# Dummy products on TensorE and earlier weight conversion in the opening of a DeltaNet and feed-forward kernel

## The chip, the cores and the metric

The kernel runs on one core of one Trainium2 chip. The metric is the device time of one execution in microseconds, the median of several runs. The engines work side by side, each through its own stream of instructions in order: TensorE (PE: matrix products; PEld: the loading of their weights), VectorE (DVE), ScalarE (ACT), GpSimd (POOL) and SyncE (SP, which issues DMAs here). TensorE's results go to PSUM, whose banks the kernel hands out in three pools.

## The reference

Two blocks follow each other. The first is a DeltaNet recurrence over 768 steps, for 4 batches and 8 heads of size 48; the second is a feed-forward block of 3072 tokens, 384 to 2048 to 384, with a sigmoid-gated activation.

```python
k_n = k / (np.linalg.norm(k, axis=-1, keepdims=True) + 1e-06)
for t in range(S):
    y[:, :, t] = np.einsum('bhd,bhde->bhe', q[:, :, t], state)
    v_old = np.einsum('bhde,bhd->bhe', state, kt)
    state = state + bt[:, :, :, None] * np.einsum('bhd,bhe->bhde', kt, vt - v_old)
...
h = x @ w_in
g = h * (1.0 / (1.0 + np.exp(-1.702 * h)))
return (g @ w_out)
```

The inputs of attention are fp32; both weight matrices reach the kernel as 64-bit floats and are converted to fp32 on the chip.

## The kernel before

**Tiling.** The sequence is cut into 6 chunks of 128 steps; a chunk of one batch (8 heads) is a unit, so there are 24 units, numbered chunk by chunk. In a unit the recurrence becomes a triangular system. Its Gram matrix of the keys is computed by `gram` (line 375: eight products into two tiles named psG, each copied to the tile G by ScalarE). The 32x32 diagonal blocks are inverted by `invert` (line 441) on VectorE, for all heads of several batches at once, in 15 growing steps of a product and a sum (tiles P and YB) and, from chunk 1 on, 8 larger ones and a pass through DRAM. In chunk 0 the last part is done by TensorE instead (`joined`, line 531: psZ, a copy by ScalarE, psC, then the tiles YT and XB on VectorE). Then the four blocks of a unit are solved one after the other.

**Hops.** `together` (line 816) is the body of a hop: for one unit, `solve` multiplies a block of V by its inverse (psU), copied to U by ScalarE; for the other, `below` multiplies the block solved in the hop before into the rows beneath (psR), which VectorE subtracts from V. Two units take turns, so that the first chunk's four units make two pairs, each with 8 hops. The first pair's hops are the loop at line 1036, the second pair's the one at line 1074. Beside each hop stands something else: the rest of `joined`, the transposes and score products of other units (psT, psQ), the Gram products of chunk 1 (`preparing`). When a pair is solved, `put_out` (line 997) computes the outputs (psY), and `state` (line 679) adds the unit's part to the state ST on VectorE (line 690) out of the same bank as part of psY. ScalarE copies psY to xT, the input of the feed-forward block. These banks and those of psU, psR and half of psQ come from one pool of four, `ps_seq`; psG of chunk 0, the products of the feed-forward block and the dummies from a pool of two, `ps_moe`.

**Dummy products.** `warm(n)` (line 132) issues n products of a 128x128 identity with 128x256 bf16 values into a tile ps_warm that nobody reads. NW = 14 stand at the very start, NY = 30 behind the Gram products (line 983), and `warm(NU // 2 if i < 6 else NA)`, 5 or 3, at the end of each hop of the first pair; NU = 11 in the first three hops of the second.

**Conversion.** `conversion` (line 205) turns a piece of a weight matrix from 64 to 32 bits in five VectorE steps (tiles w_in or w_out and tmp) and one of ScalarE. `conversions` (line 255) strings the pieces together, with the first step of a piece put among those of the piece before; `fill(n)` (line 294) issues the next n steps. The pieces of w_in come in four quarters: two pieces of 768 elements per partition, two more, three of 512, two of 768. Pieces of w_out follow, mostly of 384. When certain pieces are done, DMAs fetch more raw weights into the freed places.

**What sets the order.** The order on each engine of this part is written out by hand and kept in program order. `fill(1)` stands in each hop of the first pair, `fill(2)` behind each of its two `put_out`; `fill(2)` or `fill(3)` in each hop of the second pair, with `feed()`, which issues three products of the hidden layer (ph), from the fourth hop on; `feed()` and `fill(3)` behind each `put_out`. Then a loop (line 1097) issues two steps and one `feed()` per round until the last piece of w_in is done; then come the 25 steps of `invert(1)`, one `feed()` with each, then `fill(5)`. The rest of the conversion is issued within `both_written` (line 761, po), which waits for w_out piece by piece; from there on `woven` (line 860) interleaves the remaining units with the feed-forward block.

```python
    for i in range(2 * NB):
        together(*next(path))
        beside_hops[i]()
        fill(1)
        if i > 1:
            ahead_of(preparing, 1)
...
        warm(NU // 2 if i < 6 else NA)
    for n, s in enumerate(pair[:2]):
        put_out(s)
        load(len(KN) + n, ((KN, k),), other_queue)
        fill(2)
```

## Time and profile before

| | us |
|---|---|
| median of 3 runs | 781.13 (780.93 to 782.76) |
| the profiled execution | 784.58 |
| its span, first to last instruction | 782.9 |
| PE busy | 752.8 (96%) |
| VectorE busy | 449.1 (57%) |
| ScalarE busy | 242.0 (31%) |
| mean granted clock of TensorE | 0.964 |
| DMA moved | 50.80 MB |

The page of a profile gives the busy time of each engine, then the span in 40 slices with the busy share in tenths and the TensorE clock that was granted, in tenths of full speed. Other answers of the same trace give the busy time and the clock in any stretch, the instructions of an engine in order of time (start, duration, operation, tiles written and read, shapes, and in brackets the idle time just before with what ended it), and the chain of work that ended last, where "issue" is time in which an engine waited for nothing that the profile shows. A matrix product in fp32 appears as two records. Ends of products are modelled, so a busy PE isn't always PE at its peak.

### The profile page before, as it was taken

The numbers are of one execution on the slowest core, as the hardware profiler recorded it, in microseconds if no ns is written. First come the engines' busy times: TensorE is split into PE (matmuls) and PEld (weight loads), VectorE is DVE, ScalarE is ACT, GpSimd is POOL, SyncE is SP. The second block draws the span as 40 slices with busy tenths as digits, with TensorE's granted clock in tenths as the row PEclk, the third lists the DMA queues.
The fourth block names the chain that finished last, engine by engine and source line by source line (L and its number), as shares of the span: only waits on it lengthen the run. The fifth ranks groups of instructions, "written<-read, shape, count | busy, mean of one in ns | idle before, by whom it ended". The sixth has DMA issues, their size and how long they took to land.

```text
span 782.9 us, 19754 instructions
## 1 busy us (share of the span) xinstructions
PE 752.8 (96%) x8625; PEld 564.8 (72%) x8625; DVE 449.1 (57%) x922; ACT 242.0 (31%) x539; POOL 127.0 (16%) x133
## 2 busy tenths in 40 slices
PE   7889999688999999999999999999999999999997
PEld 5677788355678678678678678678678678687674
DVE  6747889996977666666666666666655531000000
ACT  4445652243333223223223123123123123121110
POOL 6112510011121221221221221231200000000000
PEclk8657999999999999999999999999999999999999
DMA  9931941463332141141141142142130020000000
GB/s 175 168 62 45 201 123 33 115 166 85 76 94 63 38 98 49 39 97 51 36 97 50 36 98 53 33 98 55 31 77 12 23 44 1 15 13 1 26 1 21
DMA packets 130662, 50.80 MB, mean 65 GB/s; under 512 B 105408, under 2 KB 126016, under 8 KB 130576
## 3 DMA queue, kind: packets, MB, share of 16 engines
q1 hardware_dynamic: 128112, 41.08, 23.9%
q0 software_dynamic: 2464, 8.46, 4.2%
q8 instruction: 68, 1.11, 0.6%
q14 instruction: 18, 0.15, 0.1%
HBM read 32.08 MB, written 16.25 MB: 62 GB/s over the span
## 4 chain that ended last, share of the span: by engine, by line
PE 83%; DVE 12%; issue 2%; ACT 1%; DMA 0%; POOL 0%; DVEq 0%; POOLq 0%; ACTq 0%; SPq 0%
PE po L102 29%; PE ph L102 27%; PE psU L102 6%; PE psY L102 5%; PE psQ L102 4%; PE psG L102 4%; PE psT L102 3%; DVE P L102 3%; PE ps_warm L102 2%; DVE w_out L102 2%; DVE YB L102 2%; PE psR L102 2%; DVE tmp L102 2%; DVE NT L102 1%; DVE V L102 1%
## 5 line engine op out<-in xcount | busy, mean ns | idle before, releaser
L102 PE MATMUL po<-w_out,gT 128*128 128x384 f32 x768 | 267.4, 497 | 9.6 <-ACT ksq L102 5.1
L102 PE MATMUL ph<-xT,w_in 128*128 128x256 f32 x1152 | 261.2, 383 | 0.3
L102 PEld LDWEIGHTS ph<-xT,w_in 128*128 128x128 f32 x1152 | 214.9, 190 | 32.5 <-issue 1.7
L102 PEld LDWEIGHTS po<-w_out,gT 128*128 128x128 f32 x768 | 142.0, 192 | 101.5 <-DVE w_out L102 7.8
L102 DVE TENSOR_TENSOR V<-V,psR 64x384 f32<-64x384 f32 (+1 forms) x96 | 53.3, 556 | 199.2 <-PE psR L102 198.0
L102 ACT ACTIVATE gT<-ph 128x512 f32<-128x512 f32 x96 | 56.4, 595 | 138.9 <-PE ph L102 138.8
L102 DVE TENSOR_TENSOR P<-NT,YB 64x18 f32<-64x18 f32 (+25 forms) x186 | 86.3, 464 | 5.4
L102 PEld LDWEIGHTS psU<-V,XB 32*32 32x32 f32 x1536 | 61.0, 109 | 36.8 <-issue 29.6
L102 ACT COPY US<-psU 32x384 f32<-32x384 f32 x92 | 43.2, 469 | 142.4 <-PE psR L102 124.0
L102 DVE TENSOR_REDUCE YB<-P 64x6 f32<-64x18 f32 (+25 forms) x186 | 77.7, 418 | 6.4
L102 PE MATMUL psU<-V,XB 32*32 32x48 f32 x1536 | 72.3, 208 | 2.6 <-issue 1.7
L102 PE MATMUL psR<-US,G 32*32 32x48 f32 x2208 | 64.0, 209 | 2.1 <-issue 2.1
L625 POOL TENSOR_SCALAR_AFFINE_SELECT M<-M 128x1024 f32<-128x1024 f32 x20 | 25.2, 1258 | 248.3 <-DVE M L102 170.4
L102 PEld LDWEIGHTS psR<-US,G 32*32 32x32 f32 x2208 | 54.3, 110 | 3.4 <-issue 2.8
L102 PE MATMUL psQ<-QS,kT 48*128 48x176 f32 (+1 forms) x384 | 36.2, 329 | 1.3 <-ACT QS L102 0.9
L102 PE MATMUL psG<-kT 48*128 48x128 f32 x384 | 32.5, 308 | 3.8 <-ACT kT L102 1.7
L102 PEld LDWEIGHTS psG<-kT 48*128 48x128 f32 x384 | 27.5, 208 | 7.3 <-ACT kT L102 2.1
L102 PEld LDWEIGHTS psQ<-QS,kT 48*128 48x128 f32 x384 | 29.7, 198 | 3.7 <-ACT QS L102 1.5
L102 ACT COPY o<-po 128x384 f32<-128x384 f32 x24 | 11.5, 478 | 61.8 <-issue 39.2
L102 DVE TENSOR_TENSOR P<-NT 64x256 f32<-64x256 f32 (+7 forms) x36 | 30.3, 842 | 0.4
L102 DVE TENSOR_REDUCE NT<-P 64x64 f32<-64x1024 f32 (+7 forms) x36 | 29.3, 814 | 1.2
L87 POOL DMA_DIRECT2D KN<-in_k_dram x13 | 12.4, 953 | 104.9 <-PE psY L102 96.0
(106 smaller groups left out, 629.1 us busy)
## 6 DMA issues: line engine op xcount, KB each, us to landing
Nd<-G SPq DMA_DIRECT2D x16, 512.0 KB, 3.4
V<-in_v_dram SPq DMA_DIRECT2D x24, 192.0 KB, 3.0
QP<-in_q_dram SPq DMA_DIRECT2D x24, 192.0 KB, 3.8
out_dram<-o SPq DMA_DIRECT2D x24, 192.0 KB, 2.1
KN<-in_k_dram POOLq DMA_DIRECT2D x15, 192.0 KB, 3.7
NT<-Nd SPq DMA_DIRECT2D x20, 128.0 KB, 2.6
Yd<-YS SPq DMA_DIRECT2D x20, 128.0 KB, 2.4
XB<-Yd SPq DMA_DIRECT2D x20, 128.0 KB, 3.1
```

What stands on the lines that cost most here:

```text
L87: dma(out=dst[n % len(dst)][:, :, 0:D], in_=src[b, :, c * C : (c + 1) * C, :].rearrange("h p d -> p h d"),)
L102: return lambda *a, **kw: tc.keep_in_program_order(op(*a, **kw))
L625: (pool if self.n < B else nc.gpsimd).affine_select(out=self.M, in_=self.M, compare_op=ALU.is_gt, fill=0.0, base=0, pattern=[[0, H], [1, 1 ...
```

## The change

Two things change, all of it in the first 110 us of the program. Dummy products: eight behind each of the four Gram computations of chunk 0 and eight behind the transpose of the first unit's queries, into a bank of `ps_seq`; 40 in place of 30 behind them; 11 in place of 5 in hops 0 to 5 of the first pair. Conversion: two steps in place of one in each hop of the first pair; three steps within each of the four `put_out`, between the state products and the state addition, in place of the two or three behind it. The steps themselves stay the same, and so does their order.

```diff
-    NW, NA, NY, NU = 14, 3, 30, 11
+    NW, NA, NY, NU, NG = 14, 3, 40, 11, 8
-    def warm(n, after=None):
-        ps = ps_moe.tile([128, 256], F32, tag="moe", name="ps_warm")
+    def warm(n, pool_=ps_moe, tag="moe"):
+        ps = pool_.tile([128, 256], F32, tag=tag, name="ps_warm")
...
-        def state(self, psS=None):
+        def state(self, psS=None, between=None):
...
+            if between:
+                between()
             St = ST[:, self.b, 0 : NP * D].rearrange("p (j d) -> p j d", j=NP)
             vec.tensor_tensor(St, psS, St, op=ALU.add)
...
+    def warm_beside(n):
+        warm(n, ps_seq, "seq")
+
     for b in range(HB):
         gram(b)
+        warm_beside(NG)
     pair = [new_step(n) for n in range(HB)]
+    next(pair[0].scored)
+    warm_beside(NG)
     run(pair[0].scored)
     pair[0].select()
     for b in range(HB, B):
         gram(b)
+        warm_beside(NG)
...
-        fill(1)
+        fill(2)
         if i > 1:
             ahead_of(preparing, 1)
...
-        warm(NU // 2 if i < 6 else NA)
+        warm(NU if i < 6 else NA)
     for n, s in enumerate(pair[:2]):
-        put_out(s)
+        put_out(s, lambda: fill(3))
         load(len(KN) + n, ((KN, k),), other_queue)
-        fill(2)
...
     for s in pair[2:]:
-        put_out(s)
+        put_out(s, lambda: fill(3))
         feed()
-        fill(3)
```

In the instruction order of the changed kernel the loop at line 1097 issues nothing any more, and all of its `feed()` and of the later ones, 25 in all, stand beside the inversion of chunk 1. Apart from that, only line numbers differ.

## The prediction

> **What bounds the kernel now.** I read the busy shares in slices first, then the same in stretches of 4 and 20 us, then the order of time of VectorE and TensorE between 12 and 190 us, then the chain.

> ```profile
> PE   7889999688999999999999999999999999999997
> DVE  6747889996977666666666666666655531000000
> PEclk8657999999999999999999999999999999999999
> ```

> A slice is 19.6 us. From the eleventh slice on PE is full at full clock, and the edit touches nothing there, so this steady part can't change; what can move is when it begins, about 186 us. The first four slices run at a reduced clock (0.8, 0.6, 0.5, 0.7); in slices 7 to 9 VectorE is full and PE falls to 6 and 8.

> ```profile
> 12.00:16.00 4.00, 3.13 (x85) 2.79 (x86) 3.72 (x8) 1.08 (x2) 0.97 (x2) 0.66 1.03 208
> 24.00:28.00 4.00, 3.67 (x22) 3.15 (x23) 3.86 (x5) 2.25 (x8) 1.36 (x3) 0.50 1.12 171
> 28.00:32.00 4.00, 4.00 (x33) 2.92 (x34) 3.93 (x4) 2.92 (x13) 0.00 (x0) 0.71 1.20 148
> 36.00:40.00 4.00, 3.03 (x110) 2.39 (x113) 1.41 (x3) 0.57 (x2) 0.00 (x0) 0.65 1.11 156
> 48.00:52.00 4.00, 4.00 (x124) 3.18 (x123) 1.65 (x3) 2.16 (x6) 1.09 (x1) 0.50 0.01 4
> 56.00:60.00 4.00, 4.00 (x105) 3.06 (x103) 2.33 (x6) 2.57 (x10) 1.68 (x1) 0.50 0.02 4
> 68.00:72.00 4.00, 3.65 (x80) 3.34 (x76) 3.15 (x5) 2.38 (x8) 1.94 (x3) 1.00 0.22 57
> ```

> The columns are PE, PEld, DVE, ACT, POOL, granted clock, DMA. Up to 32 us VectorE is full (the inversion of chunk 0) and PE waits for it. In the hops of the first pair (34.7 to 66 us) it is the reverse: PE 4.00 of 4.00 at clock 0.50, VectorE about half idle. In half-microsecond stretches the clock falls at 13.3, rises at 30.4, falls at 37.2, rises at 67.9.

> ```profile
> 35.31 1.66 issue
> 40.65 2.08 issue
> ```

> In the chain PE twice waits for nothing the profile shows, in hops 0 and 1; each time one of the 16 KB instruction transfers was under way while DMA was over 100% busy.

> ```profile
> 120.00:140.00 20.00, 20.00 (x94) 17.62 (x93) 18.77 (x37) 4.78 (x8) 0.00 (x0) 1.00 0.01 2
> 140.00:160.00 20.00, 12.05 (x56) 6.44 (x56) 19.42 (x35) 5.08 (x8) 1.91 (x1) 0.91 0.51 132
> 160.00:180.00 20.00, 17.98 (x178) 10.88 (x174) 19.31 (x44) 8.45 (x18) 2.96 (x2) 1.00 0.54 143
> ```

> From 105 to 141 us PE is full with the first two batches' hidden products; from 141 to 185 us VectorE (97%) sets the pace with the w_out conversion, and PE idles 5.15 us at 141.24.

> **Step 1, Gram stage: five times 8 dummies, and 40 for 30.** All of it lies in front of the first psZ, which needs the transpose YT of VectorE's inversion, 28.83 plus 1.97 = 30.80. Today PE's thirty dummies run to 32.0. A dummy took 0.213 us at 0.50 (sixteen in 26.95 to 30.36) and 0.12 at 1.00 (eleven in 1.31). Fifty more cost 6.0 us at 1.00 and 10.7 at 0.50; waits of 0.67 us three times cover 2.0. What decides is the clock. I count the time of products that fill the 128x128 array. The stretch that raised the clock at 30.4 held nothing else; the one before 67.9 held 1.11 of psT, 0.85 of dummies and most of psY's 1.87. Hop 2 (45.3 to 50.0) had 2.08 of psQ (48 of 128 rows) and 1.25 of dummies and did not rise, so narrow products count by their rows. Now 8 dummies (1.7 us) follow each gram (1.7 to 2.6 us, at 48/128), and two groups stand around a psT: 80 to 90% of a 3.4 us stretch by this count, where 66% (20.1 to 23.5 today) did not suffice and 91% did (3.05 to 6.5). I take a rise by 23.5. Then grams take 1.09 instead of 2.56, and the 40 dummies end between 29.5 and 33.3: psZ from 1.1 us earlier to 1.3 later. I take 0.

> **Step 2, the hops.** Hops 0 to 5 issue 11 dummies instead of 5: 6 x 0.213 = 1.28 us more each at 0.50 (PE is full, nothing hides it), 0.72 at 1.00. At 1.00 the rest of a hop halves (psU and psR 1.1 to 0.55, psZ or psC 1.27 to 0.65), so PE needs 0.55 + 0.65 + 1.31 = 2.5 us against today's 3.42. In hop 1, psT (1.11) and the dummies (2.35 at 0.50) stand side by side, 3.46 us of full-array products; hop 2 has psQ and 2.35. The stretch with these reaches some 80%, so I take a rise near 47 to 48 us. It stays up: 11 dummies are 1.31 of at most 3.4 us, 38% and over; stretches with as much stayed at 1.00 (72 to 79 us).

> [...]

> With the clock up, VectorE becomes the hops' bound. From the subtraction of hop 1 to the second state addition it has: subtractions 2 x 1.14 + 4 x 0.56 = 4.5; YT and XB 2 x 0.71 = 1.4; normalizing 2 x 0.54 + 0.92 = 2.0; state additions 2 x 0.36 = 0.7; 18 conversion steps on 768 elements (0.69 to 0.96, mean 0.90) and 2 on 512 (0.42) = 17.0; sum 25.7 us.

> ```profile
> 61.74 0.56 DVE L102 TENSOR_TENSOR V<-V,psR 32x384 f32<-32x384 f32 x1 [1.00 <-PE psR L102]
> 65.83 0.55 DVE L102 TENSOR_REDUCE ssq<-ksq 128x8 f32<-128x384 f32 x1
> 68.64 0.36 DVE L102 TENSOR_TENSOR ST<-psY,ST 128x192 f32<-128x192 f32 x1 [2.27 <-PE psY L102]
> ```

> The 2.27 us ahead of the first state addition now hold three steps. What waits behind these is the addition, and behind it the second pair's first psU, which needs the bank: 68.7 against 69.86 today. Hop 1's subtraction starts at 43.35 now; 1.28 of dummies more, less up to 2.08 if the instruction wait falls where PE idles anyway: 42.6 to 44.6, I take 43.8. Add 25.7 and 1.9 of waits (1.5 in hop 2, before the clock rises): second addition done at 71.4, with 22 steps done. Before stands at 73.2 with 12 (71.48 and two steps). **Gain 1.8**; bounds: loss 5 (cold throughout, rival A) to gain 7 (no waits, no instruction stall, rival C).

> **Step 3, second pair.** As many steps as before (10 + 9 + 6 = 25), in front of the additions at 102.4 and 105.4, where VectorE idled 2.26 and 0.95. PE's last psY (105.35) moves with step 2: 103.5.

> **Step 4, loop and inversion.** ("in", 3, 1) is done at step 46 (1 + 9 x 5). Before stands at 37 and makes five rounds (105.7 to 117); after stands at 47 and makes none, so 25 feeds fall beside the 25 steps of inversion. PE: from the last psY to the end of the hidden products 35.9 us (105.35 to 141.24), the same products. VectorE: psQ subtractions at about +3, inversion 27.4 (117.11 to 144.5), done at +31: the bound passes to PE. The first tail item (ssq, now 146.60 = 105.35 + 41.25) waits for ScalarE behind the last gT: 35.9 + 0.25 + 0.60 + 0.61 + 0.51 = +37.9. **Gain 3.4.** It is 0 if PE's feeds are held or the NT transfers (last issued at 110.12, 2.4 to land) stay there; 5 at best (PE's idle gap). The fetches of the weights move earlier, to a time at 0 to 2% DMA.

> **Step 5, tail.** Same steps, VectorE-bound, 0.

> Sum 1.8 + 3.4 = 5.2. The profiled execution took 784.58 (span 782.9 and 1.7 around it), so 779.4; the median of the three is 3.45 lower: 775.9, said as 776.

> **Rivals.** A, the clock stays at 0.50 through the hops (or rises after hop 4): hops 0 to 5 grow by 1.28 each, 7.7 in all; of this 2.7 return (the two steps behind the second addition, 1.9, and part of the 2.27 in front of the first); less 3.4 from step 4: +1.6, 782.7; with a late rise 778 to 780. For it: a hop of 4.7 us has only 2.35 of full-array products. Against: hops 1 and 2. B, on the other side: the Gram stage stays at 0.50. Then 10.7 less 2.0 less what 32.0 - 30.8 spares leaves psZ 7.5 late; the instruction waits (3.7) fall into that time, and the hops and step 4 are as in A: 781.1 + 7.5 - 3.7 + 1.6 = 786.5; 790 if the waits remain, 783 if the hops warm up. It decides if no stretch before 24 us raises the clock, that is if more than 90% is needed. C, more gain: the clock is up in hop 0 and neither instruction wait returns: 3.7 + 1.5 less than the forecast, 771. D, the steps do not run early since raw weights or ScalarE's part of a step are late: no gain in steps 2 to 4, 780 to 781; against it DMA at 0 to 2% from 48 us and ScalarE 2.2 of 4 busy.

> [...]

> **Numbers.** Forecast 0.50 (own range 773 to 779), A 0.19, B 0.13, C 0.13, D 0.05. 770 to 785 leaves out the ends of B and C. A difference under 0.3% (2.3 us) can't be told from none. Faster: forecast, C and the late part of A, 0.69; same 0.17; slower 0.14.

> **What would show it.** Clock 1.00 before 24 us and again by 51; hop period near 2.8 with VectorE over 85% busy from 48 to 72; state additions near 68.5 and 71; inversion's first product right behind the psQ subtractions, near 107; no PE gap at the end of ph; first po near 139.5. Wrong if the clock is 0.50 in the hops, if psZ starts after 33.5, or if the inversion waits for NT.

## The result and the profile after

The changed kernel takes 784.85 us (median of 12 executions, 781.92 to 786.86), the kernel before 782.24 beside it (780.50 to 784.17): ratio 1.003, 95% interval 1.0013 to 1.0047. A second measurement (e5 below) gave 1.0001. The forecast was 776, so the expected gain is missing; the question is where it went. The profiled execution took 786.75, its span 785.0.

The page of the changed kernel, busy tenths and granted clock in slices of 19.6 us:

```profile
PE   8697999888999999999999999999999999999997
...
DVE  6677689896977666756656666666665531000000
...
PEclk8878899999999999999999999999999999999999
```

The clock did rise: slices 2 to 4 have 0.8, 0.7 and 0.8 where before had 0.6, 0.5 and 0.7, and VectorE's third slice is a 7 where it was a 4. But PE has a 6 in the second slice and a 7 in the fourth, and the fifth slice of the clock is an 8 where it was a 9. The same stretches as before, and those where the new holes are (PE, PEld, DVE, ACT, POOL, clock, DMA):

```profile
28.00:32.00 4.00, 3.35 (x170) 2.80 (x167) 3.38 (x2) 1.37 (x6) 0.00 (x0) 1.00 1.18 149
32.00:36.00 4.00, 0.00 (x0) 0.00 (x0) 0.00 (x0) 0.00 (x0) 0.00 (x0) 0.86 0.86 146
...
48.00:52.00 4.00, 4.00 (x148) 3.50 (x142) 2.72 (x4) 2.32 (x7) 1.13 (x1) 0.94 0.13 22
...
68.00:72.00 4.00, 1.41 (x37) 1.28 (x33) 3.93 (x7) 1.48 (x5) 2.86 (x3) 1.00 0.11 27
72.00:76.00 4.00, 4.00 (x33) 3.34 (x31) 2.81 (x8) 2.68 (x8) 3.79 (x6) 0.55 0.80 249
76.00:80.00 4.00, 4.00 (x77) 3.31 (x76) 0.46 (x1) 1.48 (x3) 0.28 (x1) 0.50 1.04 270
```

At 28 us the Gram stage is warm, as forecast (1.00 where it was 0.71). Then no engine does anything between 32 and 36 us. From 48 us on the hops are warm. At 68 to 72, the border between the two pairs, VectorE works 3.93 of 4 and PE 1.41; behind that the clock is down to 0.5 and it is VectorE that idles (0.46). So there are two new holes.

**Hole 1** in the chain of waits (start, duration, what):

```profile
31.53 0.39 PE psC L102 x23
31.92 4.67 issue
36.59 0.76 PE psC L102 x38
```

PE stops in the middle of the 64 products of the first psC, for nothing that the profile shows, and VectorE's YT and XB, on which everything in hop 0 rests, wait behind it:

```profile
37.37 0.29 DVE L102 TENSOR_TENSOR YT<-YT,psC 128x128 f32<-128x128 f32 x1 [5.99 <-PE psC L102]
37.69 0.42 DVE L102 TENSOR_TENSOR XB<-YT,U 128x256 f32<-128x256 f32 x1
```

Before, the first XB stood at 34.18, 1.6 us behind the end of the inversion; now it is 6.3 us behind it. Behind PE's idle time the clock falls at 34.85, for 13.7 us.

**Hole 2**, the order of time at the border on ScalarE, PE and VectorE:

```profile
70.33 0.72 ACT L102 ACTIVATE w_in<-w_in,low 128x512 int32<-128x512 int32 x1 [2.46 <-DVE w_in L102]
...
71.11 0.54 ACT L102 COPY xT<-psY 128x256 f32<-128x256 f32 x2
...
73.06 0.54 ACT L102 COPY xT<-psY 128x256 f32<-128x256 f32 x2 [1.24 <-DVE ST L102]
```

```profile
68.29 0.65 PE L102 MATMUL psY<-US,KN 128*64 128x48 f32 x16
71.54 0.86 PE L102 MATMUL psU<-V,XB 32*32 32x48 f32 x16 [2.59 <-ACT xT L102]
72.33 2.38 PE L102 MATMUL psQ<-QS,kT 48*128 48x128 f32 x16
```

```profile
70.21 0.35 DVE L102 TENSOR_TENSOR ST<-psY,ST 128x192 f32<-128x192 f32 x1
...
79.54 1.14 DVE L102 TENSOR_TENSOR V<-V,psR 32x384 f32<-32x384 f32 x2 [4.66 <-PE psR L102]
...
86.14 1.14 DVE L102 TENSOR_TENSOR V<-V,psR 32x384 f32<-32x384 f32 x2 [3.55 <-PE psR L102]
```

The second pair's first psU waits 2.59 us, and what ends the wait is ScalarE's copy of psY to xT (71.11). Two things stand ahead of that copy. One is VectorE's addition to ST (70.21, done at 70.56), behind VectorE's three steps: the copy reads the bank that also holds the state products, and it waits for the addition, as the like copy of the second unit (73.06) shows. The other is the conversion's step in ScalarE's own queue (70.33), which waited 2.46 us for VectorE's steps. After the standstill the clock falls at 72.40 for 10.2 us, and PE's psQ and dummies run at half speed.

Further on, the inversion of chunk 1 gives back what was forecast, nearly: ssq is 38.7 us behind the last psY (41.5 before).

To compare kernels I use five marks of each trace: first XB behind the end of the inversion; hop 1's subtraction behind the first XB; the end of the second state addition behind this; the last psY of the second pair behind that; first ssq of the tail behind the last psY. All but the inversion and the addition count by their starts. Only profiled executions have them, one for each kernel. When the second state addition begins, the kernel before, e3 and e12 have done 10 steps of the conversion, e1, e7, e10 and e14 19, the others 22; so the column ST compares only kernels with equally many.

| kernel | XB | hop 1 | ST | psY | ssq | span | ratio to before, 95% |
|---|---|---|---|---|---|---|---|
| before | 1.6 | 9.2 | 28.1 | 33.6 | 41.5 | 782.9 | |
| after | 6.3 | 6.8 | 28.5 | 36.6 | 38.7 | 785.0 | 1.0030 (1.0013 to 1.0047) |
| e1 steps behind | 4.1 | 7.3 | 26.6 | 32.8 | 38.7 | 776.8 | 0.9977 (0.9951 to 1.0003) |
| e2 border dummies | 5.1 | 6.6 | 27.1 | 32.3 | 38.7 | 778.3 | 0.9979 (0.9962 to 0.9995) |
| e3 dummies only | 4.8 | 6.8 | 23.9 | 33.7 | 41.5 | 778.3 | 0.9951 (0.9936 to 0.9966) |
| e4 conversion only | 1.2 | 7.6 | 29.5 | 32.3 | 38.7 | 776.5 | 0.9966 (0.9946 to 0.9987) |
| e5 changed again | 3.3 | 6.8 | 28.6 | 34.7 | 38.7 | 781.6 | 1.0001 (0.9979 to 1.0024) |
| e6 hop dummies | 1.2 | 6.2 | 29.2 | 33.9 | 38.7 | 778.2 | 0.9997 (0.9973 to 1.0021) |
| e7 behind, kept warm | 5.0 | 6.8 | 26.6 | 33.2 | 38.7 | 780.1 | 0.9978 (0.9957 to 0.9998) |
| e8 late fetch | 5.8 | 6.8 | 29.7 | 32.3 | 38.7 | 781.8 | 1.0023 (0.9999 to 1.0047) |
| e9 wide dummies | 1.4 | 9.4 | 29.3 | 34.6 | 38.7 | 781.2 | 0.9959 (0.9933 to 0.9984) |
| e10 joined best | 1.2 | 7.4 | 25.4 | 32.8 | 38.7 | 772.7 | 0.9916 (0.9886 to 0.9947) |
| e11 copies first | 5.5 | 6.8 | 28.8 | 30.5 | 38.7 | 777.3 | 0.9948 (0.9923 to 0.9972) |
| e12 Gram dummies | 5.8 | 5.6 | 28.1 | 36.8 | 41.5 | 785.0 | 1.0026 (0.9997 to 1.0055) |
| e13 both mended | 1.2 | 7.4 | 27.3 | 32.1 | 38.7 | 774.7 | 0.9926 (0.9903 to 0.9949) |
| e14 joined, tail | 1.2 | 8.2 | 28.4 | 32.8 | 38.7 | 775.6 | 0.9923 (0.9897 to 0.9949) |

### The profile page after: what moved, and what is told of

Same layout as the page of the kernel before. It is cut to its first block, busy times and chain, and to the rows that moved or that the text cites. A ratio compares the mean times of both kernels' runs of the same rounds, so it can differ in the third digit from the quotient of the medians.

```text
span 785.0 us, 19920 instructions
## 1 busy us (share of the span) xinstructions
PE 754.9 (96%) x8711; PEld 566.3 (72%) x8711; DVE 447.2 (57%) x922; ACT 242.0 (31%) x539; POOL 127.9 (16%) x133
## 3 DMA queue, kind: packets, MB, share of 16 engines
q8 instruction: 68, 1.11, 0.6%
## 4 chain that ended last, share of the span: by engine, by line
PE 79%; DVE 15%; DMA 2%; issue 2%; ACT 1%; SPq 0%; DVEq 0%; ACTq 0%
PE po L102 29%; PE ph L102 26%; PE psU L102 6%; PE psY L102 5%; PE psQ L102 4%; DVE P L102 4%; DVE YB L102 3%; PE psG L102 3%; PE psT L102 2%; PE ps_warm L102 2%; DVE w_out L102 2%; PE psR L102 2%; DVE NT L102 1%; DVE tmp L102 1%; DVE V L102 1%
## 5 line engine op out<-in xcount | busy, mean ns | idle before, releaser
L102 PE MATMUL po<-w_out,gT 128*128 128x384 f32 x768 | 267.7, 497 | 5.8 <-DVE w_out L102 5.8
L102 PE MATMUL ph<-xT,w_in 128*128 128x256 f32 x1152 | 261.1, 383 | 0.3
L102 PEld LDWEIGHTS ph<-xT,w_in 128*128 128x128 f32 x1152 | 214.9, 190 | 32.6 <-issue 1.7
L102 PEld LDWEIGHTS po<-w_out,gT 128*128 128x128 f32 x768 | 141.9, 191 | 97.8 <-DVE w_out L102 9.0
L102 DVE TENSOR_TENSOR V<-V,psR 64x384 f32<-64x384 f32 (+1 forms) x96 | 53.4, 556 | 199.0 <-PE psR L102 197.8
L102 ACT ACTIVATE gT<-ph 128x512 f32<-128x512 f32 x96 | 56.5, 596 | 143.3 <-PE ph L102 143.2
L102 DVE TENSOR_TENSOR P<-NT,YB 64x18 f32<-64x18 f32 (+25 forms) x186 | 87.4, 470 | 5.4
L102 ACT COPY US<-psU 32x384 f32<-32x384 f32 x92 | 43.2, 470 | 141.5 <-PE psR L102 122.3
L102 PEld LDWEIGHTS psU<-V,XB 32*32 32x32 f32 x1536 | 59.2, 107 | 38.0 <-issue 28.1
L102 DVE TENSOR_REDUCE YB<-P 64x6 f32<-64x18 f32 (+25 forms) x186 | 77.7, 418 | 6.4
L102 PE MATMUL psU<-V,XB 32*32 32x48 f32 x1536 | 70.2, 205 | 4.4 <-ACT xT L102 2.6
L623 POOL TENSOR_SCALAR_AFFINE_SELECT M<-M 128x1024 f32<-128x1024 f32 x20 | 25.7, 1286 | 234.5 <-DVE M L102 168.3
L102 PE MATMUL psR<-US,G 32*32 32x48 f32 x2208 | 61.6, 207 | 0.0
L102 PEld LDWEIGHTS psR<-US,G 32*32 32x32 f32 x2208 | 52.1, 108 | 1.2 <-ACT G L102 0.5
L102 PE MATMUL psQ<-QS,kT 48*128 48x176 f32 (+1 forms) x384 | 35.1, 322 | 1.2 <-ACT QS L102 1.2
L102 PE MATMUL ps_warm<-ident 128*128 128x256 bf16 x199 | 31.5, 321 | 1.4 <-POOL ident masks.py:199 1.4
L102 PE MATMUL psG<-kT 48*128 48x128 f32 x384 | 30.1, 298 | 1.5 <-ACT kT L102 1.5
L102 PEld LDWEIGHTS psQ<-QS,kT 48*128 48x128 f32 x384 | 28.9, 192 | 3.1 <-ACT QS L102 1.8
L102 ACT COPY o<-po 128x384 f32<-128x384 f32 x24 | 11.5, 478 | 62.0 <-issue 39.5
L102 DVE TENSOR_TENSOR P<-NT 64x256 f32<-64x256 f32 (+7 forms) x36 | 30.3, 842 | 0.4
L102 DVE TENSOR_REDUCE NT<-P 64x64 f32<-64x1024 f32 (+7 forms) x36 | 29.3, 814 | 1.2
```

The costliest lines, as they stand in the source:

```text
L102: return lambda *a, **kw: tc.keep_in_program_order(op(*a, **kw))
L623: (pool if self.n < B else nc.gpsimd).affine_select(out=self.M, in_=self.M, compare_op=ALU.is_gt, fill=0.0, base=0, pattern=[[0, H], [1, 1 ...
```

## The experiments

The changed kernel once more (e5), unedited:

> The changed kernel once more, beside the others on one chip. Its twelve times lay between 781.9 and 786.9 with the mean granted clock between 0.985 and 0.970, higher clock with shorter time. If the fall of the clock at the border of the pairs is what makes it slow, the ratio to before is 1.001 to 1.005 again, and an execution with a clock of 0.983 or more shows no standstill with 0.50 behind it between 68 and 83 us. If the first result was one of that chip alone, 0.997 to 0.999.

Measured: 784.08 beside 784.42, 1.0001 (0.9979 to 1.0024). Both holes are there again. The first is smaller (the first XB 3.3 us behind the inversion); at the border psU waits as long (2.60 us), but the clock is down for 6.8 us in place of 10.2, and it is 34.7 us from the second addition to the last psY. So the change brings no gain that can be told: the two intervals together reach from 0.2% of gain to 0.5% of loss.

Three theories. **Q**: the steps put into `put_out`, with ScalarE's queue behind them, make the standstill at the border and the clock's fall after it. **D**: the dummies themselves are the price; rival to both others. **I**: the added dummies of the Gram stage are instructions, and they shift TensorE's wait for instructions into the first psC, ahead of XB.

### The two halves alone (e3, e4)

e3 takes back the conversion's part; e4 takes back the dummies.

```diff
e3, against after:
-        fill(2)
+        fill(1)
...
-        put_out(s, lambda: fill(3))
+        put_out(s, None)
...
+        fill(2)
```

(in the second pair, `fill(3)` behind `feed()`)

```diff
e4, against after:
-    NW, NA, NY, NU, NG = 14, 3, 40, 11, 8
+    NW, NA, NY, NU, NG = 14, 3, 30, 11, 8
...
-        warm_beside(NG)
...
-        warm(NU if i < 6 else NA)
+        warm(NU // 2 if i < 6 else NA)
```

> All dummies of the change, conversion steps in the places and numbers of before. Theory Q: the first pair's hops run at 1.00 from 48 us, the second pair starts at 67 to 69 with the clock up, the gain of the loop is absent: 0 to 2 us under before, ratio 0.998 to 1.000. Rival D: 3 to 5 us over before, ratio 1.004 to 1.006.

> The conversion part of the change with the dummies of before. Theory Q: the hops stay at 0.50 and take as long as before, the first psU of the second pair still waits for ScalarE until 71 to 72, the loop's gain of 2.7 us stays: ratio 0.999 to 1.003. Rival D: 5 us under before, ratio 0.993 to 0.995.

Measured: 0.9951 and 0.9966. Each half alone makes the kernel faster and both together don't, so D falls: 86 more dummies and no early steps are a gain of 0.5%. The traces show how that can be. In e4 PE is at half clock up to 67.4 us, so it comes late to the border: its last psY of the first pair ends at 68.35 and psU starts at 68.84, and it waits only 0.5 us. In e3 no steps are there, and psU follows psY at once. Where the hops are warm and the steps are there too, PE stands still for longer, 2.6 us in the changed kernel.

### The border (e1, e2, e7, e11)

e1 puts the steps behind `put_out` again. e2 leaves them and puts 24 dummies ahead of the second pair's hops. e7 has the steps behind, eleven dummies in the last two hops too, and twelve at the border.

```diff
e1, in both pairs:
-        put_out(s, lambda: fill(3))
+        put_out(s, None)
+        fill(3)
e2, ahead of the second pair's loop:
+    warm(24)
e7, e1's edit and:
-        warm(NU if i < 6 else NA)
+        warm(NU)
...
+    warm(12)
```

> The three conversion steps stand behind each put_out again, in all four places; everything else is the changed kernel. Theory Q (queue): in the changed kernel the third step's ScalarE activation stands in ScalarE's queue ahead of the copies of psY, so the second pair's first psU waits for its bank until 71.5, TensorE stands 2.8 us, the clock falls for three stretches and the second pair loses some 4.5 us. Here psU starts at 69 to 70, the clock stays at 1.00 from 48.5 us on, and the time is 4 to 5 us under the changed kernel, 2 under before (ratio 0.997). Rival D (the added dummies are the cost, wherever the steps stand): nothing changes, ratio 1.003.

> The changed kernel with 24 more dummies between the first pair's put_out and the second pair's first hop. Theory Q: psU still starts at 71.5, but TensorE is busy, the clock stays at 1.00 over 70 to 83 us, and only the cold part of the loss goes: 2 to 3 us under the changed kernel, ratio near 1.000. Rival D: more dummies, more cost, ratio 1.003 or above. If the standstill alone is the loss and not the clock: 1.003.

> The kernel with the steps behind put_out, and eleven dummies in the last two hops of the first pair too (three in the changed kernel) and twelve ahead of the second pair: nothing lets the clock fall between 48 and 105 us. Theory Q with the clock as the carrier: the spread of the kernel with the steps behind (777.2 to 785.9) closes to its lower half, 777 to 781, ratio 0.994 to 0.996. If the spread comes from elsewhere (the instruction transfers, the tail): it stays, ratio near 0.998.

Measured: 0.9977, 0.9979, 0.9978, and 32.8, 32.3 and 33.2 us in place of 36.6 from the second addition to the last psY. So either taking the standstill away or covering it with dummies brings back 3.4 to 4.3 us of that execution (1.5 to 2.4 of e5's). In e2 psU still starts 2.65 us behind the end of psY, but with dummies in that gap the clock stays up until 145 us; so what costs most is the fall of the clock behind the standstill. It stays open which of the two queues holds psU. e11 changes ScalarE's order: its copies out of psY are issued ahead of the steps and of the addition.

```diff
-                self.state(self.psS, between)
+                self.state(self.psS)
...
             act.copy(self.xT[:, 1, t], self.psY[1][:, 0, :])
+            if state and between:
+                self.add_state(self.psS, between)
```

`state` issues only the products here, `add_state` the steps and then the addition.

> The changed kernel with ScalarE's copies out of psY issued ahead of the three steps and of the state addition; on VectorE nothing moves. Theory Q in its ScalarE form (the conversion's activation stands in ScalarE's queue ahead of the copies that free the bank): the second pair's first psU starts about 1 us earlier, near 70.5 by the second state addition's time less 2.4, and the clock need not fall at the border: from the second state addition to the last psY 33 to 35 instead of 36.6, ratio 0.997 to 1.000. In its VectorE form (the state addition behind the steps holds the bank): psU as late as before, 36.6 again, ratio 1.000 to 1.004.

Measured: 0.9948. ScalarE and PE of e11 at the border:

```profile
67.97 0.54 ACT L102 COPY xT<-psY 128x256 f32<-128x256 f32 x2 [0.19 <-PE psY L102]
69.51 0.72 ACT L102 ACTIVATE w_in<-w_in,low 128x512 int32<-128x512 int32 x1 [1.00 <-DVE w_in L102]
```

```profile
68.64 0.62 PE L102 MATMUL psY<-US,KN 128*64 128x48 f32 x16
69.19 0.86 PE L102 MATMUL psU<-V,XB 32*32 32x48 f32 x16
69.98 1.60 PE L102 MATMUL psQ<-QS,kT 48*128 48x128 f32 x16
```

psU follows psY with no idle time, though VectorE still has its steps ahead of both additions (the first at 69.39, after psU had begun). No stretch at half clock follows until 152 us, psQ takes 1.60 instead of 2.38, and the last psY is 30.5 us behind the second addition. But the edit does more than reorder ScalarE's queue, and so does not tell the two queues apart. With the addition first, as in the kernel before, the copy waits for it:

```profile
69.03 0.54 ACT L102 COPY xT<-psY 128x256 f32<-128x256 f32 x2 [0.58 <-DVE ST L102]
```

This is 0.03 us behind the end of the addition (68.64 and 0.36). In e11 the copies wait for psY alone, and the addition waits for them. And psU gets another bank: in the changed kernel as it is built it takes the bank with the state products, in e11 and e13 the other one of psY; its start ahead of the addition fits that. So e11 took away both waits. How they share the 2.59 us can be estimated from the changed kernel's trace: its addition ended at 70.56, so that the copy could have begun at 70.59, and it began at 71.11. Some 0.5 us are then ScalarE's step, and 2.1 us VectorE's steps ahead of the addition. No run separates the two.

### The wait for instructions (e6, e8, e9, e12)

In e6 the Gram stage's dummies are taken back alone (NY 30, no `warm_beside`).

> The changed kernel without the dummies of the Gram stage (none behind the grams, 30 as before), with eleven per hop and all of the conversion part. Theory I (the Gram dummies harm: they move a transfer of instructions into psC of the first unit, where TensorE stood 4.67 us instead of 1.66 and 2.08): the first XB is ready at 34 instead of 36 to 38 and the time is 2 to 3 us under the changed kernel, ratio 0.999 to 1.001. Theory Q alone (the pair border): 1.003 as with them. If the Gram dummies help by an early clock: above 1.004.

Measured: the first XB 1.2 us behind the inversion in place of 6.3, as theory I has it, but a ratio of 0.9997: the standstill at the border is still there (psU waits 2.4 us, the clock is down for 3.4 us at 70.2), and e6 also does without the warm Gram stage.

e8 moves one quarter's fetch of raw weights into hop 2, to empty the DMA queues around 32 us.

```diff
-    fetch_in(2, other_queue)
+    quarter(2)
...
+        if i == 2:
+            fetch_in(2, other_queue)
```

`quarter(2)` only reserves the place of the quarter where it was reserved before.

> The changed kernel with the raw weights of the third quarter of w_in fetched from hop 2 on instead of from 16 us on, in the same places. They are read from about 70 us on. Theory I (the instruction transfer is late because the DMA engines are full until 44 us): the wait of 4.67 us in psC falls under 3, the first XB comes by 36, the time is 1 to 3 us under the changed kernel. If the wait is of the instruction stream itself: it stays at 4 to 5 us with DMA at half load, and the time too.

Measured: 1.0023, and the wait is there (XB 5.8 us behind). But the DMA share between 32 and 36 us was still 1.12, so the run did not do what it was for. Whether the wait would be shorter with idle DMA queues stays open.

e9 keeps the dummies' time and halves their instructions: one product of 128x512 values for two of 128x256 (from 28.8 us on, six of them took 1.46 us in e9, seven of the narrow ones 0.93 in the changed kernel, so 0.24 and 0.13 each). e12 is the kernel before with the Gram stage's dummies alone.

```diff
e9, against after:
-        ps = pool_.tile([128, 256], F32, tag=tag, name="ps_warm")
-        for _ in range(n):
-            pe.matmul(ps, lhsT=ones[:, 0:128], rhs=ones, start=True, stop=True)
+        ps = pool_.tile([128, 2, 256], F32, tag=tag, name="ps_warm")
+        twice = ones.rearrange("p (o n) -> p o n", o=1).broadcast_to([128, 2, 256])
+        for _ in range(n // 2):
+            pe.matmul(ps, lhsT=ones[:, 0:128], rhs=twice, start=True, stop=True)
+        for _ in range(n % 2):
+            pe.matmul(ps[:, 0], lhsT=ones[:, 0:128], rhs=ones, start=True, stop=True)
e12, against before:
-    NW, NA, NY, NU = 14, 3, 30, 11
+    NW, NA, NY, NU, NG = 14, 3, 40, 11, 8
...
+        warm_beside(NG)
```

> The changed kernel with its dummies taken two at a time: one product of 128x512 values in place of two of 128x256, so about the same time on TensorE and half as many instructions. Theory I (the extra instructions of the Gram stage move the stall that comes every 256 instructions of TensorE into the first psC): from the end of the inversion's transpose to the first XB 1.2 to 2 us instead of 6.3, the second stall elsewhere too, the clock without the fall at 34.8 or with a short one; the border unchanged (36.6 us from the second state addition to the last psY); ratio to before 0.996 to 1.000. Rival (the wait in the first psC has to do with the amount of dummy time, not with the number of instructions): 4 to 6 us there again, ratio 1.000 to 1.004.

> Before, with only the dummies of the Gram stage (five times eight and forty for thirty); five dummies per hop and the conversion as before. Theory I: the wait in the first psC rises to 3 to 5 us, hop 1's subtraction comes 1 us later than before by the end of the inversion or no earlier in spite of the clock that is up, the hops stay at half clock: ratio 1.000 to 1.005. Rival (these dummies gain by warm Gram products and the cost lies with the hops' dummies): ratio 0.995 to 0.998.

Measured: e9 0.9959, e12 1.0026. The chains of e9 and of e12:

```profile
31.45 0.66 PE psC L102 x52
32.10 0.02 issue
...
32.93 0.52 PE psU L102 x8
33.45 1.91 issue
```

```profile
31.16 0.39 PE psC L102 x23
31.55 4.12 issue
35.67 0.76 PE psC L102 x38
```

In e9 psC runs through, XB stands 1.4 us behind the inversion, and the wait comes later, in the first psU, and is shorter. In e12, which has none of the other edits, the wait is in the first psC as in the changed kernel. I counted TensorE's records (products, loads and the nine or ten of its sequencer) from the start: in every kernel the wait is ahead of number 1218, and the second wait of the kernel before is ahead of number 1474, 256 further on. With the narrow Gram dummies (after, e1, e2, e3, e5, e7, e8, e11, e12) number 1218 is in the middle of the first psC; without them or with wide ones (before, e4, e9, e10, e13, e14) in the first psU, and in e6 too, where the wait is only 0.3 us. And number 1218 began at 34.4 to 37.0 us, whatever the kernel, in all sixteen traces 1.3 to 1.7 us behind the end of a 16 KB transfer on the instruction queue that had started at 31.9 to 33.9 us. So the wait is for that transfer; in the sixteen traces the block comes at about the same time, and what the dummies decide is which instruction it holds up and how early TensorE is there. Why the transfer starts when it does stays open. XB is 3.3 to 6.3 us behind the inversion in the nine kernels of the first kind and 1.2 to 1.6 in the seven others.

e12 is not a clean price for it: in the profiled execution hop 1's subtraction was 11.3 us behind the inversion against 10.8 before, and 3.2 us more, between the second addition and the last psY, went with a stretch at half clock from 80.2 to 87.0, in the second pair: in a window in which TensorE did little more than transposes, psG and a hop's small products (0.33 by the count of the last section; the like window of before held the clock with 0.36).

The page of the changed kernel has 68 transfers of 16 KB, 1.11 MB in all, on the instruction queue for 17,422 products and loads, one for about 256. A further profiled execution of each of the two kernels agrees with the spacing: in its first 200 us every wait of TensorE over 0.3 us that nothing else explains stands at a multiple of 256 from number 1218, in the kernel before at 450 (2.73 us), 1218 (2.88) and 1474 (0.33), in the changed one at 450 (2.02), 1218 (3.01), 2242, 2498 and 2754 (0.37 to 0.43). Number 1218 began there at 38.6 and 35.5 us, 1.55 and 1.30 us behind the end of a 16 KB transfer. In all these traces TensorE stood up to 4.7 us for one of them.

### Both mended (e10, e13, e14)

e10 has e9's dummies, the first pair's steps behind `put_out`, eleven dummies in all its hops and twelve at the border. e13 is the changed kernel with e9's and e11's edits and nothing else. e14 is e10 with six dummies behind each of the first eight po products of the tail.

```diff
e10, against e9:
-        warm(NU if i < 6 else NA)
+        warm(NU)
     for n, s in enumerate(pair[:2]):
-        put_out(s, lambda: fill(3))
+        put_out(s, None)
+        fill(3)
...
+    warm(12)
e14, against e10:
             if n < FC - 1:
+                if n < 8:
+                    warm_beside(6)
                 yield 1.3
```

> The parts that were best in the runs so far, in one kernel: the dummies two at a time (as in the run beside it), the first pair's three steps behind put_out instead of within it, eleven dummies in all eight hops of the first pair, twelve more before the second pair's hops. Theories Q and I together: from inversion to hop 1's subtraction 7 to 8.5 us (before 10.8), to the second state addition 26.6, to the last psY 32.3, to the first ssq of the tail 38.7: the span some 772 to 776, ratio 0.990 to 0.995. If I is wrong: the wait in the first psC stays, 776 to 779, ratio 0.995 to 0.998. If the gains of the halves cannot be joined for another reason: 0.998 or more.

> The changed kernel with both mends: dummies two at a time, and ScalarE's copies out of psY ahead of the three steps. Everything else as in the change. If the instruction wait and the border are the whole shortfall and independent: first XB 1.2 to 2 us behind the inversion, 30.5 to 32.5 us from the second state addition to the last psY, 38.7 to the first ssq, span 772 to 777, ratio 0.989 to 0.993. If one of them hides the other or a third cause is left: 0.995 or more.

> The kernel of the tenth run with six dummies (three of 128x512) behind each of the first eight products of the first output tiles (po), where TensorE waits for the w_out conversion and the clock falls for 3.4 to 10 us at a random place. If these falls cost: no half clock between 135 and 186 us, 0.5 to 2 us less than the tenth run, ratio 0.988 to 0.992, and a smaller spread. If VectorE's conversion alone sets the pace there: as the tenth run, 0.990 to 0.994. If the dummies delay po and with it the rest: 0.994 or more.

Measured: 0.9916, 0.9926 and 0.9923; medians 777.88 (before 783.7 beside it), 776.67 and 777.43 (before 782.79). Their intervals overlap: none of the three is shown to be the best, and all beat both kernels. The slices of e13:

```profile
PE   8888999789999999999999999999999999999997
...
DVE  6788979896976665665665666666665621000000
...
PEclk8999999999999999999999999999999999999999
```

The clock is 0.9 or more in every slice but the first. e13 is the changed kernel with every step of the conversion where the change put it, and its 6.1 us of gain are a little more than the 5.2 of the forecast's sum. That they are so near is in part luck: in the profiled executions e13's last psY ends 5.8 us earlier than before (forecast 1.8), and from there to ssq it gains 2.8 (forecast 3.4). Between e9 (0.9959), e11 (0.9948) and e13 (0.9926) a plain sum of the two repairs would give 0.988 to 0.991, depending on which of the two measurements of the changed kernel one starts from; the intervals don't tell that from what was measured. In e14 no half clock is left between 50 us and the end of the conversion, and the stretch from ssq to the end of the conversion is 37.7 us, as in all kernels (37.7 to 37.8), with falls of the clock or without: there VectorE's conversion sets the pace, and a fall of the clock costs nothing.

## Why the prediction was wrong

The step that failed is the border, where step 2 hands over to step 3: the prediction has TensorE go from psY to psU without a stop, and the runs show a standstill of 2.6 us and half clock behind it. Beside it, step 1 left out where the wait for instructions would fall. Step by step:

- **Step 1** (Gram stage 0, psZ 1.1 earlier to 1.3 later): the clock rose at 17.8 (forecast: by 23.5) and psZ began at 29.73, 2.2 earlier than before, of which 1.2 is an earlier YT; as forecast or better, as far as it goes. What failed lies behind it. The prediction had seen the two waits of 1.66 and 2.08 us and read them right as far as it went (a 16 KB instruction transfer while DMA is busy; the transfers ended 0.2 and 0.3 us into the waits, and TensorE went on 1.5 and 1.7 us behind their ends), but let them only vanish or "fall into that time". It did not ask at which instruction they come, and that the dummies shift it. e9 and e12 show the shift; PE's wait grew from 1.66 to 4.67.
- **Step 2** (hop 1's subtraction at 43.8, clock up at 47 to 48, second addition at 71.4, first psU at 68.7): 44.53, 48.5, 73.0 and 71.54. The subtraction is within its bounds (42.6 to 44.6) since the earlier inversion paid for part of hole 1. From there to the addition it is 28.5 us against 27.6: VectorE was busy for 25.2 of them (forecast 25.7) and idle for 3.3 (forecast 1.9). The sentence "What waits behind these is the addition, and behind it the second pair's first psU, which needs the bank" names a chain that is there. **What failed is its price.** psU at 68.7 is 0.2 us behind the start of the first addition (near 68.5), which alone takes 0.36; the copy behind the addition, ScalarE's step ahead of that copy, and any wait of TensorE were put at nothing. In the run the addition began at 70.21, ScalarE's step held the copy until 71.11, and TensorE, done with psY at 68.94, stood for 2.59 us.
- **Step 3** (second pair moves with step 2, last psY at 103.5, so 32.1 behind the addition; the prediction counts by its end): 109.8, 36.8 behind. 4.7 us, the largest miss, and wrong in kind: the pair does not only move, it runs at half clock for 10.2 us since a standstill of 2.6 us stood in front of it. With the copies first it takes 30.8 and 32.4 (e11, e13), with dummies over the standstill 32.5 (e2).
- **Step 4** (gain 3.4): 38.7 in place of 41.5, a gain of 2.8 in every kernel with the steps early; the mechanism was right, ssq comes behind ksq (3.44 us of wait on ScalarE in the changed kernel), and the size was off: counted from the end of the last psY, as the prediction does, 38.5, 0.6 later than the 37.9 forecast.

```profile
148.32 0.55 DVE L102 TENSOR_REDUCE ssq<-ksq 128x8 f32<-128x384 f32 x1 [3.44 <-ACT ksq L102]
```

- **Step 5** (tail 0): 37.7 against 37.8; right. What lies behind the tail was 599.0 against 598.5.

The sum by marks: ssq was forecast at 146.6 - 5.2 = 141.4 and came at 148.3, so 6.9 late: 1.6 from step 2, 4.7 from step 3, 0.6 from step 4.

Of the prediction's rivals, A and B needed a cold clock in hops or Gram stage; both were warm, the hops from 48.5 us on. B's number (786.5) is near the measured one for another reason. The prediction's D (the steps do not run early) fell with the 2.8 us of step 4. C's 771 asked for warm hops with no instruction wait; e10's profiled execution, 774.4, is the nearest to it.

In the 12 executions of e12 the time goes with the mean granted clock (0.954 to 0.971 and 792.67 to 782.66 us, about 4.7 us for 0.01, correlation -0.93), in e5 more loosely (0.975 to 0.983 and 786.66 to 780.95, correlation -0.70). So part of the few us by which profiled executions and medians differ may lie in the granted clock, which no run shows by itself. The marks of one execution (e6: span 778.2, ratio 0.9997) and the ratio can therefore disagree by some us.

## What to carry to other kernels

A dummy product costs instructions as well as time. Where a trace shows TensorE waiting for its instructions, count in which product the block of instructions ends (256 in these traces) before adding any, and take the widest dummies that do. A step that is put in front of another has to be followed on every engine that it issues to, down to what frees the next bank: here the three steps delayed VectorE's addition, the copy behind it and, with one instruction in ScalarE's queue, the copy once more. A standstill costs more than its length where the clock falls behind it (here 2.6 us, and half clock for 10.2 behind them). And two edits that gain alone can lose together: the warm clock made PE early enough to meet queues that a slow PE had hardly noticed (it waited 2.59 us at the border in the changed kernel, 0.5 in e4).
